# Where the second layernorm's normalisations stand in VectorE's queue, in an attention and MLP mixer on one core

## The chip, the core and the metric

The kernel runs on one core of a Trainium2 chip. The core has a matrix engine (TensorE, PE in the profile, its weight loads PEld), a vector engine (VectorE, DVE), an activation engine (ScalarE, ACT), GpSimd (POOL) and SyncE (SP). Each engine takes its instructions in its own fixed order and waits on semaphores for the others. DMA transfers are issued from the queues of SP, POOL and ACT and run beside the engines. Matrix products accumulate in PSUM banks, which VectorE or ScalarE must empty before PE can use them again. The metric is device time in microseconds of one execution; lower is better.

## The reference, cut to what matters

```python
def _layernorm(x, axis=-1, eps=1e-5):
    m = jnp.mean(x, axis=axis, keepdims=True)
    v = jnp.var(x, axis=axis, keepdims=True)
    return (x - m) / jnp.sqrt(v + eps)

# A: 2048 queries, 32 query heads on 16 key heads of 128, window of 512 keys
q = (x @ wq)                                   # D = 576 to 32 x 128
scores = einsum("bhqd,bhkd->bhqk", q, k) * 128 ** -0.5
o = einsum("bhqk,bhkd->bhqd", softmax(scores), v)
s = o_all_heads @ wo                           # 4096 to 576
# B: an MLP with shifts, and a second one
h = gelu(_layernorm(x) @ w1); hs = shifted(h) @ w2
x1 = x + hs
B = x1 + gelu(_layernorm(x1) @ w3) @ w4        # F = 4608
# both on a layernorm of the input
xn = _layernorm(A_x)
out = A_x + A(xn) * silu(B(xn))
```

The change concerns the first `_layernorm(x)` inside B, a layernorm of `xn`, which is itself one. The kernel calls it the second layernorm; the one of x1 is its third.

## The kernel before

The 2048 tokens are cut into four blocks (`NB`) of 512, a block into four tiles (`TB`) of 128. Part A comes first, then part B.

Part A is one loop written out by hand over slots `u` from 0 (lines 724 to 747). There are `U` = 128 heads in all, 32 for each block (`Hq`), so block b begins at slot 32 b. In slot u, PE computes the scores of head u (`stage_s`, line 545, four products into `sc` banks, each followed by an exponential on ScalarE, line 549), the query of head u + 1 (`stage_q`, lines 511 and 526, into a `psq` bank, brought to `qT` by DVE on line 534 or 536), and the value products of head u - 1 (`stage_v`, line 564, twice, into the two `po` banks, each emptied by a reciprocal and a multiplication on DVE, lines 568 and 569, into `o`). SyncE then issues the DMA transposes `oT<-o` (`stage_t`, line 577). Of every four slots one computes the rests of four queries together (line 511), so that the pattern of instructions repeats with four slots.

Line 534 adds a rest to a query and is used for two of every four heads (`hh >= 2`, in slots with u % 4 equal to 1 or 2); its instruction is remembered in `behind["qT"]`. Line 536 is a plain copy, for the other two.

Work beside attention is hung into slots: `at(u, fn)` puts `fn` behind the query product of slot u, and `pe(u, atoms)` spreads matmuls over the slot. Such matmuls are the output projection of the block before (`wo_atoms`, line 269): in the slots 45 to 49, 65 to 69 and 97 to 101. A slot without one takes about 2.8 us, one with a full share about 10 us.

The second layernorm of a block is in three steps. Its statistics are taken in the slots `ln2_at`. Its normalisations (`ln2_apply`, line 209) read `xn_b[b]` and write `xm_b[b % 2]`, two instructions for each tile: one 576 columns wide and one of 64 that repeats the last columns. So blocks 0 and 2 share the buffer `xm_b0`, blocks 1 and 3 share `xm_b1`. Its transposes (`tr2`, line 260) read `xm_b` by DMA from SyncE: those of blocks 0 and 1 within the loop, in slots 67 to 70 and 71 to 74, those of blocks 2 and 3 at the beginning of part B (line 899).

The orders of SP, POOL and PE within the loop are as written (`manual_schedule` on line 723). The order of DVE and ACT is made by a scheduler, which places an instruction as soon as it is ready by its own estimate, unless `tc.issue_after(x)` keeps it behind instruction x. `tc.high_priority` lifts the instructions of attention ahead of the others. Waits follow from what is read and written: an instruction that overwrites a buffer waits for the transposes that read it.

Query weights come in pieces of four heads (`load_wq`, lines 339 and 346) from POOL's queue into two buffers in turn: piece j is issued in slot 4 (j - 1) - 1 and first used in slot 4 j - 1.

Of the kernel before, what the change touches and what calls it, by code (L numbers as in the profile page):

```python
# [31 lines left out]
def kernel(  # L32
# [21 lines left out]
    Hq = A_wq.shape[1] // Dh  # L54
# [151 lines left out]
    def ln2_apply(b, tt):  # L206
        xm, xn = xm_b[b % 2], xn_b[b]
        for dst, src in ((xm[:, tt, 0:D], xn[:, tt, 0:D]), (xm[:, tt, D:DP], xn[:, tt, NF * P:D])):
            nc.vector.tensor_scalar(out=dst, in0=src, scalar1=ln2_mv[b][:, tt, 0:1],
                                    scalar2=ln2_r[b][:, tt:tt + 1], op0=ALU.subtract, op1=ALU.mult)  # L210

    def ln2_stats_steps(b):
        hw = D // 2

        def stats(tt):
            st = small.tile([P, 2, 6], FP32, name="ln_st")
            for j in range(2):
                tc.keep_in_program_order(
                    nc.vector.bn_stats(out=st[:, j, :], in_=xn_b[b][:, tt, j * hw:(j + 1) * hw]))
            nc.vector.bn_aggr(out=ln2_mv[b][:, tt, :], in_=st[:])  # L220

        return [lambda tt=tt: stats(tt) for tt in range(TB)] + [
            lambda: rsqrt_newton(small, ln2_mv[b][:, :, 1], TB, ln2_r[b])]
# [18 lines left out]
    def late(ap, fn):  # L242
        g = nc.gpsimd.tensor_copy(out=gate[:, :], in_=ap)
        with tc.issue_after(g.ins):
            fn()
# [11 lines left out]
    def tr2(b, tt, home=None):  # L257
        if tt == 0:
            xnnT[b] = (home or stage(b))[:].rearrange("p (k t) -> p k t", k=NDC)
        nc.sync.dma_start(out=xnnT[b][:, :, tt * P:(tt + 1) * P], in_=xm_b[b % 2][:, tt, :], transpose=True)  # L260
# [38 lines left out]
    with ExitStack() as actx:  # L299
# [27 lines left out]
        def load_x(b, eng):  # L327
            x_t[b] = []
            for tt in range(TB):
                xt = xn_b[b][:, tt, 0:D]  # L330
                t = b * TB + tt
                eng.dma_start(out=xt, in_=x2[t * P:(t + 1) * P, :])
                x_t[b].append(xt)
# [83 lines left out]
        def ln1_steps(b):  # L417
            xn_t[b] = xn_b[b]
            return layernorm_steps(small, [xn_b[b][:, tt, :] for tt in range(TB)], x_t.pop(b), twice=True)
# [69 lines left out]
        def tr1(b, tt):  # L489
            transpose_tile(xT_b[b % 2], xn_t[b], tt)  # L490
# [12 lines left out]
        psq_t, rq_t, behind = {}, {}, {}  # L503
# [94 lines left out]
        def at(u, fn):  # L598
            fill.setdefault(u, []).append(fn)
# [8 lines left out]
        def later(u, make, per, pairs=False, apart=0):  # L608
            cell = []
            for i in range(2 * TB + 1):  # L610
                k = (i // 2 if i < 6 else (i - 1) // 2) if pairs else i // per
                if apart:
                    k = i // per if i <= TB else apart

                def step(i=i, k=k):
                    if not cell:
                        cell.append(make())
                    with tc.issue_after(behind["qT"].ins) if pairs and k == 1 else ExitStack():
                        cell[0][i]()
                at(u + k, step)  # L620
# [2 lines left out]
            return PLAIN - 1 <= u < U - 1 and u % 4 == 3  # L623

        ln2_at = (7, Hq + 3, 2 * Hq - 4, 2 * Hq + 20)
        tr2_at = (2 * Hq + 3, 2 * Hq + 7, 3 * Hq - 10, 3 * Hq - 5)
        WO0 = Hq + 13
        tr_k_at = {u: g for u, g in zip([*range(3, 7), *range(9, 13), *range(17, 21)], range(KDMA, Hkv))}
        x_at = (14, Hq + 14, 2 * Hq + 4)
# [5 lines left out]
        for b in range(NB):  # L635
            cell = []

            def ln2_step(i, b=b, cell=cell):
                if not cell:
                    cell.append(ln2_stats_steps(b))  # L640
                cell[0][i]()

            for i in range(TB + 1):
                at(ln2_at[b] + i // 2, lambda i=i, f=ln2_step: f(i))
            if b + 1 < NB:
                at(x_at[b], lambda b=b: late(pT_t[x_at[b]][0][0:1, 0:1], lambda: load_x(b + 1, nc.gpsimd)))
                u1 = ln1_at[b]
                later(u1, lambda b=b: ln1_steps(b + 1), 3, apart=4 if b == 1 else 0)
                for tt in range(TB):
                    at(u1 + (3 + tt, 5, 3 + tt // 2)[b], lambda b=b, tt=tt: tr1(b + 1, tt))  # L650
            for tt in range(TB):
                at(tr2_at[b] - 2 + tt // 2, lambda b=b, tt=tt: ln2_apply(b, tt))
                if b < 2:
                    at(tr2_at[b] + tt, lambda b=b, tt=tt: tr2(b, tt))
        wo_last = wo_atoms(NB - 1)[0:2]
# [94 lines left out]
    with ExitStack() as bctx:  # L750
# [144 lines left out]
        with tc.manual_schedule(engines={SP, POOL, PE, DVE, ACTE}):  # L895
# [27 lines left out]
            for k in range(len(ops) + 1):  # L923
                nxt = None
                if k < len(ops):
                    f, b, p = ops[k]
# [3 lines left out]
                if pend:  # L930
# [3 lines left out]
                    f, b, p = ops[k - 1]  # L934
# [220 lines left out]
        with tc.manual_schedule(engines={PE, DVE, ACTE}):  # L1155
# [7 lines left out]
            for d in range(0, ND, 2):  # L1163
                b = d // NP
# [56 lines left out]
            b = NB - 1  # L1221
# [15 lines left out]
        with tc.manual_schedule(engines={PE, DVE, ACTE, SP}):  # L1237
# [20 lines left out]
            tt = TB - 1  # L1258
# [22 lines left out]
    with tc.If(flag > 0):  # L1281
        nc.gpsimd.dma_start(out=g_dram[(NT - 1) * P:NT * P, :], in_=g_last)
        with ExitStack() as gctx:
# [20 lines left out]
            with tc.For_i(0, NT, 1) as t:  # L1304
# [10 lines left out]
                with tc.For_i(0, Hq, 1) as h:  # L1315
# [17 lines left out]
                    qT = work.tile([P, P], BF16, name="r_qT")  # L1333
# [62 lines left out]
```

## Time and profile before

| | us |
|---|---|
| median of 3 runs (lowest to highest) | 822.75 (822.62 to 823.31) |
| the profiled execution's own time | 823.11 |
| its span, first to last instruction | 821.5 |
| mean granted clock of TensorE | 0.996 |

The profile is one execution. Its page lists for each engine the busy time, its share of the span and the instructions. A group or wait view names a source line (L209), the tiles written and read, and a count. In the view of waits the columns are the total, the number of waits and the longest, in us. A timeline row gives the start and duration in us, the engine, line and operation, and in brackets how long the engine was idle before it and what ended that. A stretch row gives the stretch, its length, then busy time and instructions of PE, PEld, DVE, ACT and POOL, the granted clock of TensorE as a share of full speed, the mean busy share of the DMA engines and GB/s. In a view of DMA issues the last number is the median time from issue to landing in us.

### The profile page before, as it was taken

What the parts mean: (1) busy time and instruction counts of PE and PEld (TensorE: products, weight loads), DVE (VectorE), ACT (ScalarE), POOL (GpSimd) and SP (SyncE); (2) the same over time, 40 slices, a digit from 0 to 9 for tenths busy, and PEclk for the clock granted to TensorE, in tenths of its full rate; (3) what the DMA queues carried; (4) which work ended last, traced back from release to release, by engine and by line L of the source; (5) the groups of instructions that cost most, each with busy time, mean ns of one, the idle gap of its engine ahead of it and who ended that gap; (6) DMA issues with size and microseconds to landing.
All of it is one profiled execution on the core that took longest, in us unless ns stands there. A gap on an engine that the chain in (4) does not pass through costs nothing. (4 is left out here: it accounts for less than half of the span.)

```text
span 821.5 us, 19964 instructions
## 1 busy us (share of the span) xinstructions
PE 810.5 (99%) x8239; PEld 469.7 (57%) x8239; DVE 444.3 (54%) x1379; ACT 445.4 (54%) x798; POOL 125.2 (15%) x211
## 2 busy tenths in 40 slices
PE   9999999999999799999999999999999999999997
PEld 6666655466545565654665656655555555555555
DVE  6878685128822479721566528444246636655413
ACT  7888886348833588833788632033233423334520
POOL 3243231201101111100211211172000000000000
PEclk9999999999999999999999999999999999999999
DMA  8995993119732657520484462299200320330101
GB/s 213 164 206 135 184 232 81 58 33 156 159 61 59 119 113 127 114 55 14 109 125 103 79 97 64 64 317 218 77 2 16 76 60 16 48 88 16 45 15 38
DMA packets 137710, 81.26 MB, mean 99 GB/s; under 512 B 114288, under 2 KB 127888, under 8 KB 137616
## 3 DMA queue, kind: packets, MB, share of 16 engines
q1 hardware_dynamic: 123536, 39.85, 28.5%
q0 software_dynamic: 12832, 38.85, 18.3%
q8 instruction: 65, 1.06, 0.6%
q10 hardware_dynamic: 1248, 1.25, 0.5%
q14 instruction: 29, 0.24, 0.1%
HBM read 46.89 MB, written 6.93 MB: 66 GB/s over the span
## 5 line engine op out<-in xcount | busy, mean ns | idle before, releaser
L549 ACT ACTIVATE pT<-sc 128x512 bf16<-128x512 f32 x512 | 286.7, 599 | 101.9 <-PE sc L545 90.2
L545 PE MATMUL sc<-qT,kT 128*128 128x512 bf16 x512 | 171.0, 381 | 0.0
L564 PEld LDWEIGHTS <-pT 128*128 128x128 bf16 x2048 | 135.1, 98 | 57.5 <-issue 11.3
L564 PE MATMUL po<-v_sb,pT 128*128 128x129 bf16 x2048 | 159.1, 221 | 4.3 <-DVE o L569 4.2
L526 PE MATMUL psq<-xT_b,wq_b 128*128 128x512 bf16 x506 | 129.9, 379 | 0.0
L1029 PE MATMUL ph<-xT_b,w_s 64*128 64x512 bf16 x976 | 127.4, 376 | 0.0
L1066 PE MATMUL pm<-w_s,h 64*128 64x512 bf16 x864 | 122.2, 377 | 0.0
L569 DVE TENSOR_TENSOR o<-po,ri_b 128x256 bf16<-128x256 f32 x256 | 107.6, 420 | 6.6 <-DVE ri_b L568 0.3
L1047 ACT ACTIVATE h<-ph 128x512 bf16<-128x512 f32 x67 | 39.4, 597 | 132.5 <-PE ph L1029 127.7
L269 PE MATMUL pswo<-wo_sb,oT 128*128 128x512 bf16 x448 | 103.2, 379 | 0.0
L1066 PEld LDWEIGHTS <-h 64*128 64x128 bf16 x1728 | 71.1, 94 | 55.0
L269 PEld LDWEIGHTS <-oT 128*128 128x128 bf16 x1024 | 64.7, 98 | 54.2
L1066 PE MATMUL pr<-w_s,h 64*128 64x64 bf16 x864 | 90.3, 189 | 0.0
L1029 PEld LDWEIGHTS <-w_s 64*128 64x128 bf16 x1152 | 56.2, 94 | 48.2 <-issue 0.6
L526 PEld LDWEIGHTS <-wq_b 128*128 128x128 bf16 x506 | 49.5, 98 | 59.0 <-issue 1.5
L534 DVE TENSOR_TENSOR qT<-psq,rq 128x512 bf16<-128x512 f32 x62 | 42.7, 689 | 64.4 <-ACT pT L549 52.6
L536 DVE CAST qT<-psq 128x512 bf16<-128x512 f32 x64 | 43.9, 686 | 62.1 <-PE psq L511 37.5
L1045 DVE COPY hx<-ph 128x512 f32<-128x512 f32 x55 | 38.0, 691 | 60.5 <-PE ph L1029 60.5
L339 POOL DMA_DIRECT2D wq_b<-in_A_wq_dram x30 | 23.1, 769 | 273.6 <-PE sc L545 261.9
L568 DVE RECIPROCAL ri_b<-po 128x2 f32<-128x2 f32 x256 | 42.0, 164 | 38.9 <-PE po L564 34.2
L545 PEld LDWEIGHTS <-kT 128*128 128x128 bf16 x512 | 46.0, 98 | 21.0 <-DVE qT L534 0.4
L1047 ACT ACTIVATE h<-hx 128x512 bf16<-128x512 f32 x55 | 34.6, 630 | 6.2 <-DVE hx L1045 2.0
(168 smaller groups left out, 699.3 us busy)
## 6 DMA issues: line engine op xcount, KB each, us to landing
wq_b<-in_A_wq_dram POOLq DMA_DIRECT2D x30, 512.0 KB, 5.0
wo_sb<-in_A_wo_dram POOLq DMA_DIRECT2D x8, 576.0 KB, 5.4
w_s<-in_B_w_dram POOLq DMA_DIRECT2D x9, 512.0 KB, 6.1
w_s<-in_B_w_dram POOLq DMA_DIRECT2D x10, 288.0 KB, 5.1
w_s<-in_B_w_dram POOLq DMA_DIRECT2D x4, 576.0 KB, 5.4
s_b<-s_dram SPq DMA_DIRECT2D x4, 576.0 KB, 6.6
x_b<-in_A_x_dram SPq DMA_DIRECT2D x4, 576.0 KB, 7.9
out_dram<-o SPq DMA_DIRECT2D x15, 144.0 KB, 1.8
```

Source lines behind the costliest of these rows:

```text
L269: nc.tensor.matmul(ps, lhsT=oT_t[qb * Hq + h][:, tt, :], rhs=wo_sb[:, h, lo:hi], start=(i == 0), stop=(i == Hq - 1))
L526: nc.tensor.matmul(psq[:, :], lhsT=w[:, kc, hh * Dh:(hh + 1) * Dh], rhs=xT_b[qb % 2][:, kc, :], start=(kc == 0 and not (two and hh == 1)), ...
L534: behind["qT"] = nc.vector.tensor_tensor(out=qT[:, :], in0=psq[:, :], in1=rq_t.pop(u)[:, :], op=ALU.add)
L536: nc.vector.tensor_copy(out=qT[:, :], in_=psq[:, :])
L545: nc.tensor.matmul(sc[:, :], lhsT=kT[:, g, kc * P:(kc + 1) * P], rhs=qT_t[u][:, :], start=True, stop=True)
L549: behind["exp"] = nc.scalar.activation(out=pT[:, :], in_=sc[:, :], func=ACT.Exp, scale=SCALE)
L564: nc.tensor.matmul(po[:, j, :], lhsT=pTs[kc][:, tt * P:(tt + 1) * P], rhs=v_sb[:, g, kc, 0:Dh + 1], start=(kc == 0), stop=(kc == KCH - 1))
L568: nc.vector.reciprocal(out=ri, in_=po[:, :, Dh])
L569: nc.vector.tensor_tensor(out=o[:, t0:t0 + 2, :], in0=po[:, :, 0:Dh], in1=ri.unsqueeze(2).to_broadcast([P, 2, Dh]), op=ALU.mult)
L1029: nc.tensor.matmul(ps[i][:, :], lhsT=lhsT, rhs=xT[half, kc, :], start=first, stop=last, skip_group_check=True)
L1047: nc.scalar.activation(out=h3[:, :], in_=src[:, :], func=ACT.Gelu_apprx_tanh)
L1066: nc.tensor.matmul(out, lhsT=h3_t[b, fc][half, tt * P:(tt + 1) * P], rhs=w4_s[fc // WS][half, fc % WS, lo:hi], start=key not in started, s ...
```

## The change

`tr2_at` gives the slot of a block's first transpose; the normalisations of tiles 0 and 1 are hung two slots before it, those of tiles 2 and 3 one slot before it. The change moves this for blocks 2 and 3, from slots 84, 85, 89 and 90 to 97, 98, 99 and 100; blocks 0 and 1 keep 65, 66, 69 and 70. And every normalisation is now put behind the last query addition (line 534) issued when its slot is written.

```diff
         ln2_at = (7, Hq + 3, 2 * Hq - 4, 2 * Hq + 20)
-        tr2_at = (2 * Hq + 3, 2 * Hq + 7, 3 * Hq - 10, 3 * Hq - 5)
+        tr2_at = (2 * Hq + 3, 2 * Hq + 7, 3 * Hq + 3, 3 * Hq + 5)
         WO0 = Hq + 13
...
             for tt in range(TB):
-                at(tr2_at[b] - 2 + tt // 2, lambda b=b, tt=tt: ln2_apply(b, tt))
+                def apply2(b=b, tt=tt):
+                    with tc.issue_after(behind["qT"].ins):
+                        ln2_apply(b, tt)
+
+                at(tr2_at[b] - 2 + tt // 2, apply2)
                 if b < 2:
                     at(tr2_at[b] + tt, lambda b=b, tt=tt: tr2(b, tt))
```

`ln2_apply` itself is as before:

```python
def ln2_apply(b, tt):
    xm, xn = xm_b[b % 2], xn_b[b]
    for dst, src in ((xm[:, tt, 0:D], xn[:, tt, 0:D]), (xm[:, tt, D:DP], xn[:, tt, NF * P:D])):
        nc.vector.tensor_scalar(out=dst, in0=src, scalar1=ln2_mv[b][:, tt, 0:1],
                                scalar2=ln2_r[b][:, tt:tt + 1], op0=ALU.subtract, op1=ALU.mult)
```

## The prediction

> **What bounds the kernel now.** I read the page's first part, then what TensorE (PE) waited for, then the order of time around its one long wait, then the clock there.
>
> ```profile
> PE 810.5 (99%) x8239; PEld 469.7 (57%) x8239; DVE 444.3 (54%) x1379; ACT 445.4 (54%) x798; POOL 125.2 (15%) x211
> ```
>
> PE is busy for 810.5 of 821.5 us, so only its 11 us of idle time, and time at a lower clock, can be won by reordering another engine. The view of waits gives this:
>
> ```profile
> PE po L564 <- DVE o L569: 4.2, 1, 4.2
> ...
> DVE xm_b L209 <- DMA stage<-xm_b: 17.3, 4, 5.2
> ```
>
> One wait on VectorE (DVE) holds 4.2 us of it, and DVE itself waited four times, 17.3 us in all, ahead of an L209 normalisation until a transpose had read the same buffer. The timeline joins the two:
>
> ```profile
> 271.11 1.35 SPq L260 DMA_TRANSPOSE stage<-xm_b  x1
> ...
> 272.69 0.69 DVE L536 CAST qT<-psq 128x512 bf16<-128x512 f32 x1 [1.20 <-PE psq L511]
> ...
> 278.59 0.64 DVE L209 TENSOR_SCALAR xm_b<-xn_b,ln_mv,ln_r 128x576 bf16<-128x576 bf16 x2 [5.21 <-DMA stage<-xm_b]
> ...
> 279.81 1.05 PE L564 MATMUL po<-v_sb,pT 128*128 128x129 bf16 x8 [4.21 <-DVE o L569]
> ```
>
> Block 2's normalisation of its last tile overwrites xm_b0, block 0's buffer. The scheduler put it here, slot 71, although the code asks for slot 85; so it waits for block 0's fourth transpose, issued at 271.11 and landed about 278.5. Behind it in DVE's queue stand the reciprocals and o writes that empty the po banks; PE ran out of banks for 4.21 us. Then the clock:
>
> ```profile
> 279.00:280.00 1.00, 0.19 (x2) 0.19 (x3) 0.93 (x6) 0.00 (x0) 0.00 (x0) 0.82 0.00 0
> 280.00:281.00 1.00, 1.00 (x9) 0.81 (x8) 0.98 (x3) 0.00 (x0) 0.00 (x0) 0.50 0.00 0
> ...
> 282.00:283.00 1.00, 1.00 (x5) 0.41 (x3) 0.59 (x2) 0.38 (x1) 0.00 (x0) 0.50 0.31 61
> 283.00:284.00 1.00, 1.00 (x6) 0.39 (x4) 0.00 (x0) 0.71 (x2) 0.00 (x0) 0.97 0.73 140
> ```
>
> After the gap PE got 0.82, three microseconds of 0.50, and 0.97 of its clock: 0.18 + 3 x 0.50 + 0.03 = 1.71 us lost. The whole price can be measured another way, since the attention loop repeats every four slots; the L511 matmul marks each repetition.
>
> ```profile
> 272.26 0.39 PE L511 MATMUL psq<-xT_b,wq_b 64*128 64x512 bf16 x2
> ...
> 289.37 0.39 PE L511 MATMUL psq<-xT_b,wq_b 64*128 64x512 bf16 x2
> ...
> 300.55 0.39 PE L511 MATMUL psq<-xT_b,wq_b 64*128 64x512 bf16 x2
> ```
>
> ```profile
> 272.26:289.37 17.11, 12.90 (x101) 7.71 (x101) 7.69 (x22) 9.89 (x19) 1.97 (x3) 0.90 0.77 120
> 289.37:300.55 11.18, 11.18 (x102) 6.79 (x102) 7.32 (x20) 9.89 (x19) 1.97 (x3) 1.00 0.67 114
> ```
>
> Equal work took 17.11 us with the stall and 11.18 us without: 5.93 us, against 4.21 + 1.71 = 5.92. Nothing else is hidden in this period. The other three waits cost PE nothing:
>
> ```profile
> 241.97 0.64 DVE L209 TENSOR_SCALAR xm_b<-xn_b,ln_mv,ln_r 128x576 bf16<-128x576 bf16 x2 [3.96 <-DMA stage<-xm_b]
> ```
>
> ```profile
> 240.00:250.00 10.00, 10.00 (x61) 4.77 (x60) 2.52 (x7) 3.83 (x7) 0.00 (x0) 1.00 0.15 29
> 250.00:260.00 10.00, 10.00 (x60) 5.04 (x59) 2.50 (x7) 3.17 (x6) 2.37 (x5) 1.00 0.36 90
> 260.00:270.00 10.00, 10.00 (x177) 7.29 (x176) 2.83 (x8) 4.31 (x9) 0.22 (x1) 1.00 0.10 20
> ```
>
> PE is full there because those slots carry an output projection.
>
> **The change part by part.** As built, PE, ScalarE, GpSimd and SyncE keep every instruction, its order and the semaphores that it waits for; only DVE's order differs, by the same 32 L209 instructions.
>
> *Removed.* All eight L209 of block 2 leave slots 67 to 71 for slots 97 and 98, where block 0's transposes are long over. The stall goes: -4.21 - 1.71 = -5.92 us. What is late next? Nothing of PE's: the next repetition after the stall already runs at the plain 11.18.
>
> *The old places of blocks 0, 1 and 3* (block 1 about 120 us) become free:
>
> ```profile
> L209 DVE TENSOR_SCALAR xm_b<-xn_b,ln_mv,ln_r x32: 272/352/626, 41.5 to 332.8; 128x576 bf16<-128x576 bf16 x16, 128x64 bf16<-128x64 bf16 x16
> ```
>
> ```profile
> 41.78:52.96 11.18, 11.18 (x102) 6.83 (x102) 8.95 (x28) 9.89 (x19) 4.95 (x10) 1.00 1.07 213
> ...
> 322.99:334.16 11.17, 11.17 (x101) 6.82 (x101) 10.70 (x45) 9.88 (x19) 1.97 (x3) 1.00 0.85 133
> ```
>
> The periods that hold them are as short as any, so the gain there is 0.
>
> *Added in slots 65, 66, 69, 97 and 98.* A tile is a 576-wide and a 64-wide L209, 0.64 us the two (row at 241.97). Slots 65, 66, 69 and 97 take two tiles each, 1.28 us; slot 98 takes six, 3.84 us, since block 3's tie, made for slots 99 and 100, goes to an addition already past. The rows of slot 98 before:
>
> ```profile
> 360.75 0.69 DVE L534 TENSOR_TENSOR qT<-psq,rq 128x512 bf16<-128x512 f32 x1 [5.48 <-ACT pT L549]
> ...
> 364.18 0.17 DVE L568 RECIPROCAL ri_b<-po 128x2 f32<-128x2 f32 x1 [2.20 <-PE po L564]
> ...
> 370.75 0.69 DVE L536 CAST qT<-psq 128x512 bf16<-128x512 f32 x1 [5.95 <-PE psq L511]
> ```
>
> Five tiles, 3.20 us, stand ahead of the second reciprocal in place of 2.20 us of idle time: with the sixth tile around the o write, that bank is empty up to 1.7 us later, and PE comes back to it only in the next slot, after 370.75. The next query has the 5.95 us ahead of it. Cost 0; without that cover it would be 1.7 us.
>
> *Added in slot 70*, the only slot with no projection: two tiles.
>
> ```profile
> 269.59 0.69 DVE L534 TENSOR_TENSOR qT<-psq,rq 128x512 bf16<-128x512 f32 x1 [3.25 <-PE psq L526]
> ...
> 273.93 0.60 PE L545 MATMUL sc<-qT,kT 128*128 128x512 bf16 x2
> ```
>
> They take 1.28 us where DVE was idle for 1.20 (row at 272.69), so the next query leaves DVE at about 273.5 in place of 273.4. The first matmul that needs it is the second of the pair at 273.93. Bounds: 0 and the whole 1.28 if nothing hid it. I take 0.
>
> *Waits added on SyncE.* Block 0's transposes must now follow normalisations in slots 65 and 66.
>
> ```profile
> 237.59 0.42 DVE L569 TENSOR_TENSOR o<-po,ri_b 128x256 bf16<-128x256 f32 x1
> ...
> 239.32 1.27 SPq L260 DMA_TRANSPOSE stage<-xm_b  x1
> ```
>
> The first went out at 239.32, behind slot 66's last o write, which stands behind those four tiles in DVE's order. Queued behind it are only oT transposes for a projection some 30 slots later. Cost 0. The GpSimd queue is not touched.
>
> *Sum.* 823.11 (the profiled execution's own time) - 5.92 = 817.19. That execution lay 0.36 above the median of 822.75, so 816.83 beside the runs; I say 816.9 us.
>
> [...]
>
> **The rivals.**
>
> *The clock term is not there in ordinary runs.* Then only 4.21 is won: 822.75 - 4.21 = 818.54. [...] Against: the three runs and the profiled one lie within 0.7 us, less than 1.71. Chance 6%.
>
> *Slot 70 is too full.* PE is held for up to the 1.28: 816.83 + 1.28 = 818.1. Against it is the gap from 273.5 to the pair at 273.93. 5%.
>
> *The stall returns on another wait; the change does not do what it says.* In slots 70 and after, o writes now show waits of their own for the transposes that last read their buffers.
>
> ```profile
> 210.46 28.80 SPq L577 DMA_TRANSPOSE oT<-o  x14
> ```
>
> ```profile
> DMA to landing us min/median/max: 2.6/3.8/12.2
> ```
>
> Slot 71's o write needs head 52's, the first of those 14, all out by 239.3; even with 12.2 us, the longest landing of an xm_b transpose, that is 251.5, well ahead of 271. If it held all the same, 5.92 us come back: 822.75. 4%.
>
> *Slower: a late query weight.* Slot 70's normalisations run while GpSimd issues the wq piece that slot 75 uses first.
>
> ```profile
> 270.53 1.21 POOL L346 DMA_DIRECT2D wq_b<-in_A_wq_dram  x2
> ...
> 288.41 1.03 PE L526 MATMUL psq<-xT_b,wq_b 128*128 128x512 bf16 x4
> ```
>
> ```profile
> wq_b<-in_A_wq_dram POOLq DMA_DIRECT2D x2, 32.0 KB, 6.4
> ```
>
> It landed by 271.74 + 6.4 = 278.1; with the stall gone PE wants it at 288.41 - 5.92 = 282.5, a margin of 4.4. From a landing past 288.4 the change loses. At three times 6.4 it is 291.0: 8.5 us of wait and 1.71 of clock, 816.83 + 10.2 = 827.0.
>
> ```profile
> 30.05 1.53 POOL L362 DMA_DIRECT2D v_sb<-in_A_v_cache_dram  x2
> ```
>
> ```profile
> 42.01 1.49 POOL L362 DMA_DIRECT2D v_sb<-in_A_v_cache_dram  x2
> ```
>
> Against it: the issues at 42.01 ran beside block 0's L209 and took 1.49, not more than the 1.53 elsewhere. 3%. [...]
>
> **How the numbers follow.** Forecast 82% (816.4 to 817.4: the runs' spread of 0.7 about 816.9), rivals 6, 5, 4 and 3%. The range takes in 818.54 and a little below the forecast's spread: 816.2 to 818.7, leaving out 7% and some edge. A difference of 0.2%, 1.65 us, is about what a measurement of this kernel tells from none. Faster: 82 + 6 + 5 = 93%; same 4%; slower 3%.
>
> **What would show it.** Right: no DVE wait on a stage transpose, no PE wait on o, clock 1.00 from slot 70 to 76, an L511 period of 11.2 after 272.26, and L209 near 225, 234, 263, 270, 345 and 355 us. A PE gap in slot 71 speaks for the full slot, one in slot 75 before L526 for the late weight, a DVE wait ahead of L569 for the returned stall. Wrong would be a time above 818.7 or a new gap of PE over 1 us.

## The result and the profile after

The changed kernel takes 817.51 us (median of 6 runs, 817.06 to 818.12) against 823.15 us for the kernel before (6 runs, 822.62 to 826.47). The ratio is 0.9926, 95% interval 0.991 to 0.9943. The profiled execution of the changed kernel took 817.43 us, with a span of 815.8 us and a mean granted clock of 0.999. Line numbers after 654 are 4 higher than before.

The page of the changed kernel and its view of waits:

```profile
PE 803.9 (99%) x8157; PEld 467.2 (57%) x8239; DVE 445.5 (55%) x1379; ACT 445.4 (55%) x798; POOL 125.3 (15%) x211
```

```profile
PE warm L687 <- POOL ident masks.py:199: 1.9, 1, 1.9
PE warm L690 <- DVE nr_y L450: 0.8, 1, 0.8
PE psq L526 <- DMA wq_b<-in_A_wq_dram: 0.2, 1, 0.2
PE pm L269 <- issue: 0.2, 1, 0.2
```

VectorE does the same 1379 instructions in nearly the same time (445.5 us, before 444.3). The wait of `po` for `o` is gone from PE's list, and no row of VectorE waits for `stage<-xm_b` any more. PE's busy time is 6.6 us lower with equal work, but 82 records of matmuls are missing from this profile (8157 of 8239), so that difference is not read further; the periods below are.

The timeline of the changed kernel at slots 70 and 71, and the stretches of the two periods from there:

```profile
270.10 0.69 DVE L534 TENSOR_TENSOR qT<-psq,rq 128x512 bf16<-128x512 f32 x1 [3.25 <-PE psq L526]
270.70 0.45 DVE L209 TENSOR_SCALAR xm_b<-xn_b,ln_mv,ln_r 128x576 bf16<-128x576 bf16 x1
...
271.61 1.35 SPq L260 DMA_TRANSPOSE stage<-xm_b  x1
...
272.41 0.29 DVE L209 TENSOR_SCALAR xm_b<-xn_b,ln_mv,ln_r 128x64 bf16<-128x64 bf16 x1
272.77 0.39 PE L511 MATMUL psq<-xT_b,wq_b 64*128 64x512 bf16 x2
273.19 0.69 DVE L536 CAST qT<-psq 128x512 bf16<-128x512 f32 x1 [0.49 <-PE psq L511]
...
274.44 0.59 PE L545 MATMUL sc<-qT,kT 128*128 128x512 bf16 x2
```

```profile
272.77:283.95 11.18, 11.07 (x100) 6.80 (x102) 7.32 (x20) 9.89 (x19) 1.97 (x3) 1.00 1.09 170
283.95:295.12 11.17, 11.06 (x99) 6.78 (x100) 7.32 (x20) 9.88 (x19) 1.97 (x3) 1.00 0.68 128
```

Block 1's normalisations, which had been done about 120 us into the kernel, now stand behind the query addition of slot 70. VectorE's idle time ahead of the next query copy is 0.49 us instead of 1.20. That copy still begins 0.42 us after the L511 matmul (272.77 to 273.19; before, 272.26 to 272.69), and the matmul pair that needs the query 1.67 us after it (274.44; before, 273.93). The period is 11.18 us at full clock, where it was 17.11 at 0.90.

### The profile page after: what moved, and what is told of

It is laid out like the page before. It is cut to its first block, busy times and chain, and to the rows that moved or that the text cites. A ratio compares the mean times of both kernels' runs of the same rounds, so it can differ in the third digit from the quotient of the medians.

```text
span 815.8 us, 19889 instructions
## 1 busy us (share of the span) xinstructions
PE 803.9 (99%) x8157; PEld 467.2 (57%) x8239; DVE 445.5 (55%) x1379; ACT 445.4 (55%) x798; POOL 125.3 (15%) x211
## 3 DMA queue, kind: packets, MB, share of 16 engines
q8 instruction: 65, 1.06, 0.6%
## 5 line engine op out<-in xcount | busy, mean ns | idle before, releaser
L545 PE MATMUL sc<-qT,kT 128*128 128x512 bf16 x507 | 168.4, 379 | 0.1
L526 PE MATMUL psq<-xT_b,wq_b 128*128 128x512 bf16 x451 | 121.8, 379 | 3.1 <-DMA wq_b<-in_A_wq_dram 0.2
L269 PE MATMUL pswo<-wo_sb,oT 128*128 128x512 bf16 x434 | 101.2, 379 | 0.6
L516 ACT ACTIVATE rq<-sc 128x512 f32<-128x512 f32 x62 | 33.6, 594 | 8.4 <-PE sc L511 8.4
```

The costliest lines, as they stand in the source:

```text
L269: nc.tensor.matmul(ps, lhsT=oT_t[qb * Hq + h][:, tt, :], rhs=wo_sb[:, h, lo:hi], start=(i == 0), stop=(i == Hq - 1))
L526: nc.tensor.matmul(psq[:, :], lhsT=w[:, kc, hh * Dh:(hh + 1) * Dh], rhs=xT_b[qb % 2][:, kc, :], start=(kc == 0 and not (two and hh == 1)), ...
L545: nc.tensor.matmul(sc[:, :], lhsT=kT[:, g, kc * P:(kc + 1) * P], rhs=qT_t[u][:, :], start=True, stop=True)
```

## The experiments

Time went from one place, so the questions were which half of the change does it, what made that one wait so long, how much room slot 71 has, and whether the clock's part of the loss is a fixed price.

### The tie without the new slots, and the new slots without the tie

`e1_tie_only` is the changed kernel with the old slots:

```diff
-        tr2_at = (2 * Hq + 3, 2 * Hq + 7, 3 * Hq + 3, 3 * Hq + 5)
+        tr2_at = (2 * Hq + 3, 2 * Hq + 7, 3 * Hq - 10, 3 * Hq - 5)
```

> Every normalisation tied behind a query addition, the slots of before (84, 85, 89 and 90 for blocks 2 and 3). Theory (the stall is a wait that stood too early in DVE's queue; the tie alone moves it): no DVE wait on a stage transpose, the L511 period from 272 is 11.2 us, 817.5 us, as with the whole change. Rival (plain slots of that stretch, where DVE is 98% busy, have no room for block 2's four tiles, 2.56 us of DVE): the stall goes but up to 2.6 us come back there, 818.5 to 820.1 us.

Measured: 817.14 us (816.77 to 817.76; ratio 0.9921, 0.9904 to 0.9938). The period after the L511 matmul of slot 71, of this kernel:

```profile
272.83:284.01 11.18, 11.07 (x100) 6.79 (x102) 7.31 (x20) 9.88 (x19) 1.97 (x3) 1.00 1.09 180
```

`e2_slots_only` is the kernel before with the new slots:

```diff
-        tr2_at = (2 * Hq + 3, 2 * Hq + 7, 3 * Hq - 10, 3 * Hq - 5)
+        tr2_at = (2 * Hq + 3, 2 * Hq + 7, 3 * Hq + 3, 3 * Hq + 5)
```

> Blocks 2 and 3 in the new slots, no tie. Theory: the scheduler still places block 2 as soon as its statistics are there, the 4.2 us wait of PE and the halved clock stay, 822.8 us. Rival (the move to the projection's slots is what helps): 817.5 us.

Measured: 823.58 us (822.44 to 825.91; ratio 1.0001, 0.9985 to 1.0017). Its timeline:

```profile
279.14 0.64 DVE L209 TENSOR_SCALAR xm_b<-xn_b,ln_mv,ln_r 128x576 bf16<-128x576 bf16 x2 [5.11 <-DMA stage<-xm_b]
...
280.37 0.63 PE L564 MATMUL po<-v_sb,pT 128*128 128x129 bf16 x8 [4.11 <-DVE o L569]
```

The slots where the code asks for a normalisation do nothing by themselves: the scheduler hoists it into slot 71 all the same. The tie does everything, and it does so at the old slots too. The rival of the tie alone, no room in the plain slots there, falls: none of its periods between two L511 marks is as much as 0.05 us longer than before.

### Block 2 alone

`e4_block2_only` is the kernel before with the new slots and the tie for block 2 only; blocks 0, 1 and 3 stay where the scheduler had put them.

```diff
-        tr2_at = (2 * Hq + 3, 2 * Hq + 7, 3 * Hq - 10, 3 * Hq - 5)
+        tr2_at = (2 * Hq + 3, 2 * Hq + 7, 3 * Hq + 3, 3 * Hq - 5)
...
+                    with tc.issue_after(behind["qT"].ins) if b == 2 else ExitStack():
+                        ln2_apply(b, tt)
```

> The kernel of before with the change applied to block 2 alone (its new slots and its tie); blocks 0, 1 and 3 stay where the scheduler put them. Theory (block 2's last tile is all that cost; the moves of the other blocks are worth 0): the period from 272 is 11.18 us and the time that of the whole change, 817.5 us, within 0.3. Rival (the moves of the other three blocks free or load DVE enough to matter): the time lies more than 0.5 us from that of the whole change.

Measured: 817.05 us (816.84 to 817.38; ratio 0.9911, 0.9888 to 0.9934). Moving 8 of the 32 instructions wins as much as moving all of them. The other 24 cost nothing and gain nothing that these runs can tell.

### What the wait consists of: the shared buffer, and the store ahead of the transpose

`e3_own_buffer` is the kernel before, with block 2's last tile in a buffer of its own (and one `o` buffer fewer, to make room). Nothing is tied.

```diff
+    xm2_t = keep.tile([P, DP], BF16, name="xm2_t")
...
+        xm = xm2_t if (b, tt) == (2, TB - 1) else xm_b[b % 2][:, tt, :]
```

> The kernel of before, but block 2's last tile is normalised into a buffer of its own (the o pool has 17 buffers in place of 18 to make room). Nothing is tied. Theory (the cost is the wait for the transpose that read the shared buffer): the three harmless waits of 4 us stay, the one in slot 71 goes, PE idles under 0.5 us there, clock 1.00, 817.5 us. Rival (the early place in DVE's queue costs by itself): PE still waits about 4 us on o in slot 71, 822.8 us.

Measured: 817.33 us (816.88 to 817.81; ratio 0.9926, 0.9909 to 0.9942). PE has no wait on `o`; VectorE's view of waits still shows three waits of this kind, in slots where PE has other work:

```profile
DVE xm_b L211 <- DMA stage<-xm_b: 12.4, 3, 4.5
```

`e5_store_late` is the kernel before, with the store of block 1's output projection, which SyncE issues just ahead of block 0's last transpose, moved from slot 69 to slot 80.

```diff
-                if qb < NB - 1:
+                if qb < NB - 1 and qb != 1:
                     store()
+                if qb == 1:
+                    late_store[0] = store
...
+        at(2 * Hq + 16, lambda: late_store[0]())
```

> The kernel of before, but block 1's store of s (576 KB), which left SyncE just ahead of block 0's last transpose, is issued in slot 80. Theory (that transpose landed 7 us after its issue because the store and its queue stood ahead of it): it is issued near 268 us and lands within 3 us, DVE's fourth wait shrinks below 2 us, PE does not wait, 817.5 us. Rival (any such wait in DVE's queue in a plain slot costs PE its 4 us, whatever the traffic): 821 to 823 us.

Measured: 817.14 us (817.01 to 821.26; ratio 0.9932, 0.9912 to 0.9953; five of the six runs are at most 817.41, and why one took 821.26 is not known). Its timeline and its waits:

```profile
268.83 1.27 SPq L260 DMA_TRANSPOSE stage<-xm_b  x1
271.48 0.45 DVE L209 TENSOR_SCALAR xm_b<-xn_b,ln_mv,ln_r 128x576 bf16<-128x576 bf16 x1 [1.14 <-DMA stage<-xm_b]
```

```profile
DVE xm_b L209 <- DMA stage<-xm_b: 13.5, 4, 4.4
```

All four waits on the buffer are still there, but the harmful one lasts 1.14 us: the transpose is issued at 268.83 instead of 271.11, and has landed 2.6 us later, where before it took 7.4 us (271.11 to about 278.5). So the long wait needs both the shared buffer and the store's place ahead of the transpose. How the store lengthens it is not shown. Without the store the transpose also goes out ahead of a query weight's 512 KB (that load is issued at 269.84; before, at 269.78, ahead of the transpose), and a transpose was slower beside such a load without any store too: 2.6 us for block 1's transpose issued at 284.23 in the kernel before, 5.4 for the one issued at 287.26, behind a weight load of 286.89:

```profile
stage<-xm_b SPq DMA_TRANSPOSE x1, 2.6
```

```profile
stage<-xm_b SPq DMA_TRANSPOSE x1, 5.4
```

The normalisation also moved in this build (it waits from 270.34 on, before from 273.38), so the length of the wait is not the transpose's alone.

### How much room slot 71 has

Dead statistics on VectorE were put into the changed kernel between the query copy and the reciprocals of slot 71, where the old normalisation had stood: n = 3, 6, 8 and 10. Their results are not used.

```diff
-                    nc.vector.tensor_copy(out=qT[:, :], in_=psq[:, :])
+                    behind["copy"] = nc.vector.tensor_copy(out=qT[:, :], in_=psq[:, :])
...
+        def filler(n=6):
+            f = small.tile([P, n, 6], FP32, name="fill", bufs=1)
+            with tc.high_priority(offset=HP), tc.issue_after(behind["copy"].ins):
+                for i in range(n):
+                    nc.vector.bn_stats(out=f[:, i, :], in_=xn_b[0][:, 0, 0:512])
+
+        at(2 * Hq + 7, filler)
```

> The changed kernel with 3 dead bn_stats of 512 columns, about 0.6 us each, put on DVE in slot 71 between the query copy and the reciprocals, where the wait stood before. In the profile of before a delay of 5.7 us there left PE idle for 4.21, so 1.5 us of it is slack. Theory: 1.8 us of filler leave PE idle 0.3 us, clock 1.00, a period of 11.5 us, 817.8 us. Rival (no slack in a plain slot): 1.8 us more, 819.3 us.

> The same with 6, about 3.6 us. [...] Rival (any gap of PE halves the clock for 3.4 us): a period of 15.0 us, 821.3 us.

> The same with 10, about 6.0 us. [...] Rival (the low clock in the profile of before had another cause than the gap): the clock stays at 1.00, a period of 15.7 us, 822.0 us.

> The changed kernel with eight dead statistics operations on VectorE between the query copy and the reciprocals of slot 71; they leave work in that nobody uses. Six of them left TensorE idle for 1.92 us at full clock, ten for 4.29 us at half clock; eight, 8 x 0.602 = 4.8 us, should leave it idle for about 3.1 us. Theory (the clock falls only when TensorE's idle time is over some length between 1.92 and 4.11 us, and the loss of the clock is a step): at 3.1 us either the clock stays at 1.00 and the query's period is 11.18 + 3.1 = 14.3, the time 817.4 + 3.1 = 820.5; or it falls whole and the period is 16.0 to 17.1, the time 822.3 to 823.3. Rival (the loss of the clock grows in proportion to the idle time): the period is 14.3 + 1.3 = 15.6 and the lowered clock shows for about 2.5 us.

The period is the distance from the L511 matmul of slot 71 to the next one.

| fillers | time, us (lowest to highest) | filler row, us | PE's wait for `o`, us | period, us | over 11.18 + wait |
|---|---|---|---|---|---|
| 3 | 818.26 (817.67 to 819.27) | 1.87 | none listed | 11.49 | 0.31 |
| 6 | 819.07 (818.80 to 819.67) | 3.65 | 1.92 | 13.26 | 0.16 |
| 8 | 822.06 (820.67 to 823.28) | 4.83 | 3.10 | 16.13 | 1.85 |
| 10 | 824.18 (822.83 to 825.93) | 6.02 | 4.29 | 18.25 | 2.78 |

PE's first matmul after the gap, in the timelines of the kernels with six, eight and ten:

```profile
277.38 0.63 PE L564 MATMUL po<-v_sb,pT 128*128 128x129 bf16 x8 [1.92 <-DVE o L569]
```

```profile
278.41 0.63 PE L564 MATMUL po<-v_sb,pT 128*128 128x129 bf16 x8 [3.10 <-DVE o L569]
```

```profile
279.59 1.05 PE L564 MATMUL po<-v_sb,pT 128*128 128x129 bf16 x8 [4.29 <-DVE o L569]
```

Three fillers, 1.87 us, cost 0.3; from six on each further us on VectorE costs PE one: 1.18 us more row from six to eight lengthens the wait by 1.18, 1.19 more to ten by 1.19. Of 1.87 us some 1.56 are covered, of 3.65 us 1.57 (3.65 - 13.26 + 11.18): VectorE can be about 1.6 us late in this slot before PE's period grows. In these profiles, one of each kernel, the clock's part in the last column comes out as a step: 0.16 after 1.92 us of idle time, 1.85 after 3.10. The proportional rival, 15.6 and a low clock of 2.5 us for eight fillers, is wrong: it was 16.13 and 3.4 us. The rivals with six and ten fall too: 13.26, not 15.0, and 18.25 with a lowered clock, not 15.7. (With three, the profiled execution, the one of 819.27 us, also waited 1.9 us for a late query weight in slot 19, of which more below.)

The clock itself, in one-microsecond stretches of the kernels with eight and ten fillers:

```profile
278.00:279.00 1.00, 0.59 (x9) 0.57 (x10) 1.00 (x3) 0.00 (x0) 0.00 (x0) 1.00 1.32 260
279.00:280.00 1.00, 1.00 (x12) 0.70 (x10) 0.93 (x5) 0.60 (x1) 0.00 (x0) 0.86 0.10 18
280.00:281.00 1.00, 1.00 (x4) 0.29 (x2) 0.38 (x1) 0.96 (x2) 0.00 (x0) 0.50 0.61 123
...
282.00:283.00 1.00, 1.00 (x8) 0.72 (x7) 0.69 (x1) 0.40 (x1) 0.00 (x0) 0.50 0.49 98
283.00:284.00 1.00, 1.00 (x14) 0.83 (x13) 0.58 (x2) 0.60 (x2) 0.00 (x0) 0.94 0.30 61
```

```profile
278.00:279.00 1.00, 0.00 (x0) 0.00 (x0) 1.00 (x4) 0.00 (x0) 0.00 (x0) 0.58 0.38 70
279.00:280.00 1.00, 0.41 (x4) 0.41 (x5) 1.00 (x6) 0.00 (x0) 0.00 (x0) 0.50 0.00 0
...
284.00:285.00 1.00, 1.00 (x6) 0.45 (x5) 0.40 (x1) 0.04 (x1) 0.00 (x0) 0.51 0.53 106
285.00:286.00 1.00, 1.00 (x18) 0.88 (x16) 0.76 (x3) 0.84 (x2) 0.00 (x0) 1.00 0.84 162
```

A share of 0.86 in a stretch means 0.28 us at half clock, so with eight fillers the clock is low for 0.28 + 3 + 0.12 = 3.4 us and PE loses 1.70. With ten it is low from about 278.2, while PE is still idle, to 285.0: 6.8 us, twice as long, of which PE works in 5.4 and loses 2.7.

### Both kernels once more

The kernels before and after were profiled again, unchanged.

> The kernel before, profiled once more, unchanged. Theory: TensorE's wait for VectorE's o is there again with 4.1 to 4.2 us. If the length of the lowered clock depends on when the idle time falls, the stretch at 0.50 is 3.4 us in one execution and up to 6.8 us in another, and the period after the stall is 17.1 to 18.2; rival: the idle time alone sets it, and the period is 17.1 as in the first profile.

> The changed kernel, profiled once more, unchanged. Theory: the wait of the projection for wq_b in slot 19 is of varying length from execution to execution, since it is the landing of one transfer (7.3 to 12.2 us in the profiles so far): 0 to 1.9 us, here with a period of 11.2 to 13.3 that ends near 64; all other periods stay at 11.17 to 11.26. Rival: it belongs to the changed kernel, and is 0.2 with a period of 11.60 as before.

The kernel before (824.15 us):

```profile
279.73 0.64 DVE L209 TENSOR_SCALAR xm_b<-xn_b,ln_mv,ln_r 128x576 bf16<-128x576 bf16 x2 [5.08 <-DMA stage<-xm_b]
...
280.95 0.63 PE L564 MATMUL po<-v_sb,pT 128*128 128x129 bf16 x8 [4.09 <-DVE o L569]
```

```profile
273.52:290.64 17.12, 12.93 (x100) 7.39 (x102) 7.59 (x22) 9.89 (x19) 1.97 (x3) 0.90 0.73 116
```

```profile
PE psq L526 <- DMA wq_b<-in_A_wq_dram: 1.4, 1, 1.4
```

The stall and its period are the same as in the first profile, 17.12 against 17.11; this execution did not show a longer stretch at half clock. It does show the query weight of slot 19 late by 1.4 us, which the first profile did not. In the second profile of the changed kernel (818.91 us) that wait is there too:

```profile
64.53 1.04 PE L526 MATMUL psq<-xT_b,wq_b 128*128 128x512 bf16 x3 [1.07 <-DMA wq_b<-in_A_wq_dram]
65.54 0.71 PE L511 MATMUL psq<-xT_b,wq_b 64*128 64x512 bf16 x2
```

So this wait belongs to neither kernel: 0 and 1.4 us before, 0.2 and 1.1 us after. It was 1.9 us with three fillers, and the other profiles do not list it. The rival that tied it to the changed kernel falls.

`e8_wo_later` is the changed kernel with another load moved away from that piece:

```diff
-        for i, u in enumerate((13, 21, 25, 29, 33, 36, 38, 41)):
+        for i, u in enumerate((23, 21, 25, 29, 33, 36, 38, 41)):
```

> The changed kernel with the first load of the output projection's weight moved from slot 13 to slot 23, away from the query weight's piece that is issued in slot 15 and first used in slot 19. Theory (the two loads share the DMA engines): the piece lands within 8 us instead of 9.9 to 12.2, there is no wait for wq_b, and the period that ends near 64 is 11.2: the time is 0 to 0.5 us below that of the changed kernel, about 817.1, which is hardly more than its runs differ by. Rival (the landing is set by x's loads or varies for another reason): the piece lands in 9 to 12 us still and the time is 817.4 or more.

Measured: 817.07 us (816.86 to 817.69; ratio 0.9926, 0.991 to 0.9942). The DMA issues from 50 to 58 us, of the second profile of the changed kernel and of this one:

```profile
wq_b<-in_A_wq_dram POOLq DMA_DIRECT2D x1, 512.0 KB, 11.4
...
wq_b<-in_A_wq_dram POOLq DMA_DIRECT2D x2, 32.0 KB, 11.5
```

```profile
wq_b<-in_A_wq_dram POOLq DMA_DIRECT2D x1, 512.0 KB, 6.6
wq_b<-in_A_wq_dram POOLq DMA_DIRECT2D x2, 32.0 KB, 6.7
```

The piece lands within 7 us and the wait is gone in this execution. That the moved load did it is not shown: with the load where it was, the piece also landed in 6.8 us (the kernel with a buffer of its own) and in 7.0 us (the new slots alone), so its landing varies for another reason besides, which stays open; and 817.07 against 817.51, with ranges that overlap, is not a difference that these runs settle. The times of the tie alone (817.14) and of block 2 alone (817.05), with the load where it was, lie as low.

## Why the prediction was right, and where it was off

*The stall's removal, -4.21 - 1.71 = -5.92.* Right, in size too. The period went from 17.11 to 11.18, which is 5.93, and the kernels without the tie (17.14) and with it (11.18) show that nothing else in the change does this.

*Nothing of PE's is late next.* Right: the period after it, 11.17, is plain, and so are all later ones.

*Old places of blocks 0, 1 and 3, gain 0.* Right: block 2 alone gives the whole gain.

*Slots 65, 66, 69, 97 and 98, cost 0.* Right. The rows of slots 65 and 98, with the query behind it, in the changed kernel:

```profile
225.53 1.18 DVE L209 TENSOR_SCALAR xm_b<-xn_b,ln_mv,ln_r 128x576 bf16<-128x576 bf16 x4
...
356.93 2.26 DVE L209 TENSOR_SCALAR xm_b<-xn_b,ln_mv,ln_r 128x576 bf16<-128x576 bf16 x8
359.10 0.16 DVE L568 RECIPROCAL ri_b<-po 128x2 f32<-128x2 f32 x1
...
365.33 0.69 DVE L536 CAST qT<-psq 128x512 bf16<-128x512 f32 x1 [5.19 <-PE psq L511]
```

Two tiles take 1.18 us, not 1.28. The last o write of slot 98 comes 4.19 us after the slot's query addition, before 3.63: 0.56 us later, where the prediction allowed 1.7. The query after slot 98 still has 5.19 us of idle time ahead of it.

*Slot 70, cost 0 within 0 to 1.28.* Right at the lower bound: the next query is not even the expected 0.1 us later. The fillers show a margin behind it as well, about 1.6 us in the slot that follows.

*Waits added on SyncE, 0.* Right: block 0's last transpose is issued 1.16 us ahead of the L511 matmul (271.61 to 272.77), before 1.15 (271.11 to 272.26).

*The sum.* From 823.11 it gave 817.19, and the profiled execution took 817.43. Of the 30 periods between L511 marks only two differ by 0.05 us or more between the first profiles of the two kernels: the one from slot 71, 5.93 shorter, and the one that ends at 64.63 us, 11.60 instead of 11.18, 0.42 longer for the late query weight, which comes and goes in both kernels. What lies ahead of the first mark is 0.07 longer, what follows the last 0.26 shorter. That makes 5.70, the difference of the two spans, 821.5 and 815.8, and leaves no other cost or gain in the loop. The last step, 0.36 off for the distance of the profiled execution to the median of three, was mis-sized: with six runs beside the changed kernel the median before is 823.15, and 823.15 - 5.92 = 817.23 would have been 0.3 closer to 817.51 than the 816.9 that was forecast. The 817.51 lies inside the range, but 0.1 above the 816.4 to 817.4 to which the forecast's 82% belonged.

*Why the clock term was held to be there.* Here the reason was weaker than the conclusion. The prediction argued from runs within 0.7 us. Beside the experiments there are 45 executions of the kernel before with the clock recorded, from 820.59 to 827.83 us. By mean granted clock:

```
clock   runs   mean time, us
0.998     9    822.50
0.997     9    822.97
0.996     9    823.39
0.995    15    824.69
```

The other three are one at 0.999 (821.72), one at 0.994 (827.53) and one at 0.993 (827.83). This mean holds more than the stall: the first profiles of both kernels end with a low stretch after the last matmul, where it costs PE nothing. In the first profile of the kernel before, whose last matmul ends at 816.81:

```profile
818.00:819.00 1.00, 0.00 (x0) 0.00 (x0) 0.00 (x0) 0.00 (x0) 0.00 (x0) 0.97 0.10 21
819.00:820.00 1.00, 0.00 (x0) 0.00 (x0) 0.00 (x0) 0.00 (x0) 0.00 (x0) 0.50 0.16 33
```

Of the span it takes 2.5 us at half clock here, 1.9 in the first profile of the changed kernel and, by a mean of 1.0, at most 0.8 in the second: up to 0.0015 of the mean; the stall's 1.71 us are 0.0021. So one low stretch of 3.4 us in the loop reads as 0.998 to 0.996, and the 17 executions at 0.995 or less probably lost more, like the profiled one with ten fillers, which was low for 6.8 us in the loop and reads 0.995. This is an estimate from the profiles; the kernel before has no profile at so low a clock. They took 2.3 us longer on average than the 18 at 0.997 and 0.998. So the clock's loss does not look like a constant 1.71 but varies from execution to execution. It is not the whole spread: the nine at 0.998 alone reach from 820.59 to 824.60, and what differs among them stays open. The changed kernel has 0.999 or 1.0 in all six runs, and a spread of 1.06 us; its two profiles have no low stretch but the one at the end.

*The rivals.* The clock term was there in ordinary runs: 817.51 against the rival's 818.54, and only one of the 45 executions before at 0.999. The stall did not return, slot 70 is not too full, and the query weight of slot 75 was not late. A late query weight did occur, but in slot 19, by up to 1.4 us before and 1.1 after, and so not through this change; the gap over 1 us that it makes is not a new one. The changed kernel's issue row beside L209 in slot 70:

```profile
271.04 1.24 POOL L346 DMA_DIRECT2D wq_b<-in_A_wq_dram  x2
```

It took 1.24 us where it had taken 1.21, and the period that uses this piece is plain: that the normalisations beside it hold up this issue is not shown.

## What to carry to other kernels

When a bound engine has one long wait, follow it to the instruction that stands at the head of the other engine's queue, and see whether that instruction was needed there: here a normalisation due 14 slots later waited 5.21 us for a buffer and held the evictions behind it, and with them PE for 4.21 us. Naming a later slot did not move it, because the scheduler places what its own estimate calls ready; a dependence on a late enough instruction did. To price such a stall, compare equal periods of the loop (17.11 and 11.18 us here); that includes the clock's part.

## What the hardware showed that was not expected

*The clock was halved with a gap of 3.10 us too, and the halving began before or after PE resumed.* With eight fillers PE resumed at 278.41 and the clock fell at about 279.7, 1.3 us later; with ten it fell at about 278.2, 1.4 us before PE resumed at 279.59. In the two profiles of the kernel before it fell 0.2 us before PE resumed and 1.3 us after. The gap of 1.92 us left it at full speed. No gap between 1.92 and 3.10 us was measured in this slot, and the same fillers may come out either way: one run with eight had a mean clock of 0.999 and took 820.67 us, where 817.51 + 3.10 without a clock term is 820.61, while the others had 0.995 to 0.998.

*The low stretch came in lengths of 3.4 and 6.8 us.* In the first profile of the kernel before the clock was at half for 3.41 us, from 279.64 on, and with eight fillers for 3.4. With ten it was 6.8 us, the first 1.4 of them while PE was still idle. In the 3.4 us ahead of the fall PE had been idle for 3.4 us (the kernel before), 2.1 (eight fillers) and 2.9 (ten). What sets the moment of the fall, and what the length, is not shown.
